# A linear-attention block on one core: a re-ordered head, later weight loads, and another column order for the folded kv product

## The chip, the cores and the metric

The kernel runs on one core of a Trainium2 chip. The metric is the device time of one execution in microseconds (us). A profiled execution also gives a span (first to last instruction); times are about 1.7 us longer than spans. The other cores are idle.

Every run also reports its mean granted TensorE clock (1.0 is full speed). For one core, a run is labelled slow only when it is over 1.5% above the fastest run of the same kernel; the means below use the other runs, called fast.

## The reference

Only the first block and the input of the second matter. S is 2048 tokens, D is 640, 32 heads of 20.

```python
xn = layernorm(x)                              # [2048, 640]
q, k, v = split(xn @ wqkv)                     # 32 heads of 20
pq, pk = phi(q), phi(k)                        # phi(t) = t+1 for t>0, else exp(t)
kv  = einsum("hsd,hse->hde", pk, v)            # 20 x 20 per head
den = einsum("hsd,hd->hs", pq, pk.sum(s))
o   = einsum("hqd,hde->hqe", pq, kv) / den
A   = o @ wo
B   = x + scatter(8 chosen tokens, gated MLP of them)   # chosen by x @ w_r
return x + A + B                               # block B on layernorm(x) too
```

The kernel never forms v or o. It accumulates G = xn^T pk over all tokens, gets kv from G and wv, keeps only the 20x20 blocks by a mask, and folds kv into wo: M = kv wo. The output is then pq M.

## The kernel before

Tokens come in 16 tiles of 128. For each tile t: load x, statistics (`ln_stats`), the power 0.5 on GpSimd, normalise (`ln_xn`), transpose (by TensorE for tiles 0 to 2, by DMA for the rest), key products `K(t)`, two activations `PHa`, a min-add `PHb` on VectorE, and the accumulation `G(t)`. I count tiles from 0.

```python
    def ln_mid(t, on_act=True):
        ...
        dve.tensor_scalar(out=t2[:], in0=MV[:, t, 1:2], scalar1=EPS_BF16, scalar2=None, op0=ALU.add)
        pool.tensor_tensor(out=s[:], in0=t2[:], in1=halfc[:], op=ALU.pow)
        ...
    def tr_dma(t):
        sp.dma_start_transpose(xnT[:, :, t * P : (t + 1) * P], XX[:, t, 0, :])
    def PHb(t):
        ek, rk = phis[t]
        dve.scalar_tensor_tensor(out=pk[:, t, :], in0=ek[:], scalar=1.0, in1=rk[:], op0=ALU.min, op1=ALU.add)
    ...
    def loads(t):                       # called at the end of iteration t, all on one queue but wo2
        if t < 5:
            ld(sp, XX[:, 6 + 2 * t : 8 + 2 * t, 1, :], x_v[:, 6 + 2 * t : 8 + 2 * t, :])
        if 5 <= t < 10:  ...            # one fifth of wq
        if 7 <= t < 12:  ...            # one fifth of wv
        if t == 9 or t == 10:  ...      # half of wo1
        if t == 13:  ...                # wg, in five
        if t == 14:  ...                # wu, in five
    ...
    def kv_ev(b0, b1):                  # mask kv on its way out of PSUM, columns re-ordered
        k1 = kv1[:].rearrange("p m g q -> p g q m")
        k2 = kv2[:].rearrange("p m g q -> p g q m")
        m1 = bm1[:].rearrange("p (q m) -> p q m", m=KC)
        for g in range(NG):
            src = PS[:, b0, g * GC : (g + 1) * GC] if g < 3 else PS[:, b1, 0:GC]
            dve.tensor_tensor(out=k1[:, g], in0=src.rearrange("p (q m) -> p q m", m=KC), in1=m1, op=ALU.mult)
        src = PS[:, b1, GC : 2 * GC].rearrange("p (q m) -> p q m", m=KC)
        for g in range(NG):
            dve.tensor_tensor(out=k2[:, g], in0=src, in1=bm2[:, g, :].rearrange("p (q m) -> p q m", m=KC), op=ALU.mult)

    def m_main(m, b, eng):              # one of five parts of M
        for h in range(2):
            for g in range(NG):         # narrow products: 32 output rows each
                pe.matmul(PS[32 * g : 32 * g + 32, b + h, 0:HW], lhsT=kv1[:, m, g, :], rhs=wo1[:, g, h * HW : (h + 1) * HW], ...)
            pe.matmul(PS[:, b + h, 0:HW], lhsT=kv2[:, m].rearrange("p g q -> p (g q)"), rhs=wo2[:, h * HW : (h + 1) * HW], ...)
        ...
    # ---- the order around the folding
    kv_pe(3, 6)
    kv_ev(3, 6)
    q_pe(0, 4, 1)                       # PE work that stands ahead of the first folded product
    q_fin(0, 3)
    zmask(4)
    q_pe(1, 0, 2)
    q_fin(0, 4)
    m_main(0, 6, dve)
```

## Time and profile before

131.05 us, median of three runs (130.75 to 131.63). The profiled run took 131.35 us with a span of 129.6 and a mean clock of 0.974.

| stretch (us from the span's start) | what | PE busy | VectorE busy |
|---|---|---|---|
| 0 to 27 | head, until the tiles follow each other freely | 21.6 of 27 | 20.4 |
| 27 to 57 | tile loop | 28.6 of 30 | 20.7 |
| 66 to 72 | masking of kv | 3.5 of 6 | 5.9 |
| 77 to 126 | rest of q, the output | all | 32.8 |

TensorE (PE) is the engine to feed. The key products of tiles 3, 4, 5, 6 and 15 start at 18.28, 22.01, 25.52, 28.19 and 54.00 us; when nothing waits, they are 2.67 us apart.

From the page of the kernel before: busy time of PE, then rows of 40 equal slices of the span (3.24 us each) in tenths of busy time; PEclk is the granted clock in tenths.

```profile
PE 117.0 (90%) x943; PEld 66.5 (51%) x943; DVE 90.5 (70%) x210; ACT 82.0 (63%) x184; POOL 21.9 (17%) x56
...
PE   6779887899998979999994799999999999999990
...
PEclk9986999999999999999999869999999999999999
DMA  3980068986487996999991000000000022222223
```

Counting slices from 0, PE has dents in slices 0 to 6 and in 21 and 22; around each there are two slices of lower clock (2 and 3, 22 and 23). The smaller dents in slices 12 and 14 are waits for late transposes in the loop. DMA is busy all through the loop, up to slice 20.

The waits of PE, from the view of who waited for whom (total us, times, longest):

```profile
PE PS L588 <- DVE kv L583: 2.5, 1, 2.5
PE PS L197 <- DMA xnT<-XX: 1.9, 3, 0.8
PE PS L174 <- DVE XX L167: 1.4, 2, 0.9
```

The largest is one wait of the first folded product (line 588) for the masking of kv (line 583). Key products (line 197) wait three times for DMA transposes. The view of the transposes' line gives their times from issue to landing:

```profile
DMA to landing us min/median/max: 2.6/2.9/4.6
```

The busy time per stretch puts the dents and the clock side by side. Columns: stretch, its length, busy us (and instructions) of PE, PE's weight loads, VectorE, ScalarE, GpSimd, then granted clock, DMA share and GB/s.

```profile
core 0: us, PE busy (x) PEld busy (x) DVE busy (x) ACT busy (x) POOL busy (x), PEclk, DMA share, GB/s
5.36:8.77 3.41, 1.54 (x12) 0.76 (x12) 2.96 (x12) 1.30 (x4) 0.56 (x1) 0.97 1.01 264
8.77:12.18 3.41, 3.41 (x17) 2.17 (x18) 3.08 (x11) 1.46 (x6) 0.55 (x1) 0.53 0.16 59
66.00:72.00 6.00, 3.53 (x46) 2.10 (x44) 5.92 (x9) 2.30 (x5) 0.00 (x0) 1.00 0.37 134
69.90:73.30 3.40, 1.29 (x12) 0.66 (x12) 3.40 (x7) 0.76 (x2) 0.00 (x0) 1.00 0.00 0
73.30:76.72 3.42, 3.42 (x34) 1.15 (x32) 2.80 (x10) 1.50 (x3) 0.21 (x1) 0.52 0.03 7
```

After 3.4 us in which PE was busy less than half the time (1.54 and 1.29 us), its clock is 0.53 and 0.52 in the next 3.4 us. (The stretches are cut by eye; under a_oldkv the halved ones are placed more exactly, at 8.54 and 73.40 us.) The groups of the folding (busy us, mean ns of one, idle time before):

```profile
L588 PE MATMUL PS<-wo,kv 128*32 128x320 bf16 x40 | 3.5, 337 | 2.5 <-DVE kv L583 2.5
L591 PE MATMUL PS<-wo,kv 128*128 128x320 bf16 x10 | 3.4, 337 | 0.0
L583 DVE TENSOR_TENSOR kv<-PS,bm 128x160 bf16<-128x160 f32 x4 | 3.2, 1083 | 0.0
L580 DVE TENSOR_TENSOR kv<-PS,bm 128x160 bf16<-128x160 f32 x4 | 3.0, 1050 | 0.2 <-PE PS L566 0.2
```

Eight multiplications of only 160 elements per partition take over 1 us each.

### The profile page before, as it was taken

Reading aid. Unit: us, or ns where it says so; the run is one execution under the profiler, and the core shown is the slowest. Engines: PE = TensorE matmul, PEld = TensorE weight load, DVE = VectorE, ACT = ScalarE, POOL = GpSimd, SP = SyncE. Lnnn points to the kernel's source line nnn. Section 1 sums busy time; section 2 is a strip of 40 time slices with the busy share of each in tenths; the row PEclk is TensorE's granted clock in tenths of the full one; section 3 lists DMA queues with packets and bytes.
Section 4 is the critical chain, followed back from the end, with each engine's and each line's share of the span. In section 5 each row is a group of like instructions: output and inputs, shape, how many; then the busy total and the mean of one; then the engine's idle time right before and its main releaser. Section 6 shows DMA issues by size and latency. Waiting matters only on the chain.

```text
span 129.6 us, 2638 instructions
## 1 busy us (share of the span) xinstructions
PE 117.0 (90%) x943; PEld 66.5 (51%) x943; DVE 90.5 (70%) x210; ACT 82.0 (63%) x184; POOL 21.9 (17%) x56
## 2 busy tenths in 40 slices
PE   6779887899998979999994799999999999999990
PEld 2246544466664546664572244464554565666660
DVE  1887987987999773247789954588568786855551
ACT  3055585868988674537946075788988879993000
POOL 7211337753332140000000014000000000000000
PEclk9986999999999999999999869999999999999999
DMA  3980068986487996999991000000000022222223
GB/s 89 347 223 0 0 149 201 162 199 135 94 216 168 223 248 110 333 364 413 309 347 37 5 3 0 0 8 3 0 0 5 0 108 94 106 101 104 101 101 101
DMA packets 20861, 16.87 MB, mean 130 GB/s; under 512 B 10512, under 2 KB 19568, under 8 KB 20848
## 3 DMA queue, kind: packets, MB, share of 16 engines
q1 hardware_dynamic: 18096, 15.24, 41.8%
q10 hardware_dynamic: 2752, 1.47, 4.4%
q8 instruction: 7, 0.11, 0.4%
q14 instruction: 6, 0.05, 0.1%
HBM read 11.80 MB, written 2.62 MB: 111 GB/s over the span
## 4 chain that ended last, share of the span: by engine, by line
PE 62%; DVE 20%; DMA 10%; ACT 2%; issue 2%; POOL 1%; SPq 0%; DVEq 0%; POOLq 0%; ACTq 0%
PE PS L664 18%; PE PS L447 16%; PE PS L197 8%; DMA xnT<-XX 7%; PE PS L228 4%; DVE pk L223 4%; DMA XX<-in_A_x_dram 3%; DVE XX L167 3%; DVE stats L143 3%; DVE kv L580 2%; DVE stats L141 2%; DVE kv L583 2%; PE PS L588 2%; PE PS L591 2%; PE PS L655 2%
## 5 line engine op out<-in xcount | busy, mean ns | idle before, releaser
L197 PE MATMUL PS<-wk,xnT 128*128 128x320 bf16 (+1 forms) x160 | 26.0, 311 | 3.6 <-DMA xnT<-XX 1.9
L447 PE MATMUL PS<-xnT,wq 128*128 128x512 bf16 x100 | 25.0, 389 | 0.0
L664 PE MATMUL PS<-Mb,pqT 128*128 128x320 bf16 x160 | 23.8, 300 | 0.0
L228 PE MATMUL PS<-pk,XX 128*128 128x512 bf16 x80 | 23.3, 379 | 0.5 <-DVE pk L223 0.5
L197 PEld LDWEIGHTS <-xnT 128*128 128x128 bf16 x160 | 15.6, 101 | 12.4 <-DMA xnT<-XX 3.8
L215 ACT ACTIVATE ek<-PS 128x320 bf16<-128x320 f32 x32 | 14.2, 444 | 12.2 <-PE PS L197 10.8
L223 DVE SCALAR_TENSOR_TENSOR pk<-ek,rk 128x640 bf16<-128x640 bf16 x16 | 13.1, 818 | 8.5 <-ACT rk L216 8.4
L453 ACT ACTIVATE qe<-PS 128x512 bf16<-128x512 f32 x20 | 11.9, 595 | 10.7 <-PE PS L447 6.5
L664 PEld LDWEIGHTS <-pqT 128*128 128x128 bf16 x160 | 14.7, 97 | 6.9 <-issue 0.2
L682 DVE TENSOR_TENSOR o<-PS,XX 128x640 bf16<-128x640 f32 x15 | 12.4, 824 | 7.8 <-PE PS L664 7.0
L459 DVE SCALAR_TENSOR_TENSOR pqT<-qe,qr 128x512 bf16<-128x512 bf16 x20 | 13.7, 694 | 2.3 <-ACT qr L454 2.1
L447 PEld LDWEIGHTS <-wq 128*128 128x128 bf16 x100 | 11.0, 120 | 8.4 <-issue 1.0
L216 ACT ACTIVATE rk<-PS 128x320 bf16<-128x320 f32 x32 | 14.3, 447 | 0.0
L153 POOL TENSOR_TENSOR s<-t,halfc 128x1 bf16<-128x1 bf16 x16 | 9.4, 586 | 27.5 <-DVE t L152 21.7
L233 PE MATMUL PS<-pk,XX 128*128 128x128 bf16 x64 | 14.0, 219 | 0.0
L190 ACT ACTIVATE XX<-XX,MR,SR 128x640 bf16<-128x640 bf16 x16 | 13.6, 913 | 0.0
L155 ACT ACTIVATE c<-XX,MV 128x640 bf16<-128x640 bf16 x13 | 11.1, 854 | 1.9 <-DVE MV L144 1.8
L228 PEld LDWEIGHTS <-XX 128*128 128x128 bf16 x80 | 7.8, 98 | 8.4 <-issue 0.3
L454 ACT ACTIVATE qr<-PS 128x512 bf16<-128x512 f32 x20 | 11.8, 591 | 0.0
L141 DVE BATCH_NORM_STATS2 stats<-XX 128x6 f32<-128x320 bf16 x16 | 7.8, 486 | 2.4 <-DMA XX<-in_A_x_dram 2.4
L143 DVE BATCH_NORM_STATS2 stats<-XX 128x6 f32<-128x320 bf16 x16 | 7.8, 485 | 0.0
L167 DVE TENSOR_SCALAR XX<-c,SR 128x640 bf16<-128x640 bf16 (+2 forms) x17 | 6.3, 377 | 1.5
(129 smaller groups left out, 122.9 us busy)
## 6 DMA issues: line engine op xcount, KB each, us to landing
out_dram<-o SPq DMA_DIRECT2D x15, 160.0 KB, 1.8
wg<-in_B_w_gate_dram SPq DMA_DIRECT2D x5, 384.0 KB, 4.7
wu<-in_B_w_up_dram SPq DMA_DIRECT2D x5, 384.0 KB, 7.9
wd<-in_B_w_down_dram SPq DMA_DIRECT2D x1, 1920.0 KB, 9.3
XX<-in_A_x_dram SPq DMA_DIRECT2D x5, 320.0 KB, 3.6
wk<-in_A_wqkv_dram ACTq DMA_DIRECT2D x2, 400.0 KB, 5.1
wq<-in_A_wqkv_dram SPq DMA_DIRECT2D x5, 160.0 KB, 2.7
wv<-in_A_wqkv_dram SPq DMA_DIRECT2D x5, 160.0 KB, 2.8
```

Source lines behind the costliest of these rows:

```text
L190: act.activation(XX[:, t, 1, :], XX[:, t, 1, :], AF.Identity, bias=MR[:, t : t + 1], scale=SR1[:, t : t + 1])
L197: pe.matmul(PS[:, b + h, 0:w], lhsT=xnT[:, kc, t * P : (t + 1) * P], rhs=wk[:, kc, h * HW : h * HW + w], start=(kc == 0), stop=(kc == KC - 1),
L215: act.activation(ek[:, sl], PS[:, b + h, 0:HW], AF.Exp)
L216: act.activation(rk[:, sl], PS[:, b + h, 0:HW], AF.Relu)
L223: dve.scalar_tensor_tensor(out=pk[:, t, :], in0=ek[:], scalar=1.0, in1=rk[:], op0=ALU.min, op1=ALU.add)
L228: pe.matmul(PS[:, a, :], lhsT=lhsT, rhs=pk[:, t, 0:512], start=(t == 0), stop=(t == T - 1),)
L233: pe.matmul(PS[:, 5, a * P : (a + 1) * P], lhsT=lhsT, rhs=pk[:, t, 512:D], start=(t == 0 and a == 0), stop=(t == T - 1), skip_group_check= ...
L447: pe.matmul(PS[:, bank, :], lhsT=by5(wq[:, kc, :])[:, m, :], rhs=xnT[:, kc, tb * TBLK : (tb + 1) * TBLK], start=(kc == 0), stop=(kc == KC ...
L453: act.activation(e, PS[:, bank, :], AF.Exp)
L459: dve.scalar_tensor_tensor(out=pqT[:, m, tb * TBLK : (tb + 1) * TBLK], in0=e, scalar=1.0, in1=r, op0=ALU.min, op1=ALU.add,)
L664: pe.matmul(PS[:, b + h, 0:HW], lhsT=pqT[:, kc, t * P : (t + 1) * P], rhs=Mb[:, kc, h * HW : (h + 1) * HW], start=False, stop=(kc == KC - ...
L682: dve.tensor_tensor(out=ot[:].rearrange("p (h c) -> p h c", h=2), in0=PS[:, b : b + 2, 0:HW], in1=XX[:, t, 1, :].rearrange("p (h c) -> p h ...
```

## The change

The intent: keep kv in natural column order, so that its masking is three contiguous instructions, and let the folded product read its weights with a step of five columns instead; keep weight loads out of the loop, where they meet the DMA transposes; normalise tile 0 before the statistics of tile 1, transpose tile 3 by PE too, and put small filler products into PE's gaps so that its clock stays up. Smaller parts: `w_r` is loaded as five rows and transposed by PE instead of as a column of 2-byte pieces, and a copy of the mean disappears by storing the statistics in the upper half of float32 words.

```diff
     def kv_ev(b0, b1):
-        (eight multiplications with a re-ordered output, as above)
+        dve.tensor_tensor(out=kv1[:, 0:3, :], in0=PS[:, b0, 0 : 3 * GC].rearrange("p (g c) -> p g c", c=GC),
+                          in1=bm1[:].unsqueeze(1).to_broadcast([P, 3, GC]), op=ALU.mult)
+        dve.tensor_tensor(out=kv1[:, 3, :], in0=PS[:, b1, 0:GC], in1=bm1[:], op=ALU.mult)
+        dve.tensor_tensor(out=kv2[:], in0=PS[:, b1, GC : 2 * GC].unsqueeze(1).to_broadcast([P, NG, GC]),
+                          in1=bm2[:], op=ALU.mult)
     def m_main(m, b, eng):
         for h in range(2):
             for g in range(NG):
-                pe.matmul(..., lhsT=kv1[:, m, g, :], ...)
+                pe.matmul(..., lhsT=by5(kv1[:, g, :])[:, m, :], ...)
-            pe.matmul(PS[:, b + h, 0:HW], lhsT=kv2[:, m].rearrange("p g q -> p (g q)"), ...)
+        for h in range(2):
+            pe.matmul(PS[:, b + h, 0:HW], lhsT=by5(kv2[:].rearrange("p g c -> p (g c)"))[:, m, :], ...)

     def loads(t):
         if t < 5:  ...                                   # x, unchanged
-        (wq, wv, wo1, wo2 in pieces at t = 5 to 11; wg at 13; wu at 14)
+        if t == 13:                                      # behind the last tr_dma(15)
+            ld(sp, wq[:], ...); ld(sp, wv[:], ...); ld(sp, wo1[:], ...); (wo2, wg, wu)

+    (head written out by hand; its start)
+    ln_xn(0, ((0, 3 * P), (3 * P, D)))
+    warm(1, 256)                                         # filler products of 256 columns
+    tr_pe(0, 0, act, act)
+    warm(3, 256)
     ln_stats(1, 0)
-    ln_xn(0, ((0, 3 * P), (3 * P, D)))
-    tr_pe(0, 0, act, act)
...
+    warm(3, 256)
+    tr_pe(1, 2, act, act)
...
+    tr_pe(3, 3, act, act)                                # tile 3 by PE, before by DMA
... (cut: w_r by rows, MVf, where constants are made)
```

More of the change, by code (lines that the diff above doesn't have):

```diff
@@ L90 @@
     rbf = st([P, T], BF16, "rbf")
-    MV = st([P, T, 2], BF16, "MV")
+    MVf = st([P, T, 2], F32, "MVf")
+    MV = MVf[:].bitcast(BF16).rearrange("p t (k o) -> p t k o", o=2)[:, :, :, 1]
     SR = st([P, T], F32, "SR")
@@ L104 @@
     dve.memset(zero[:], 0.0)
+    dve.memset(MVf[:], 0.0)
     ld(act, wk[:, :, 0:HW], wqkv_v[:, :, D : D + HW])
@@ L107, with warm @@
     ld(act, wk[:, :, HW:D], wqkv_v[:, :, D + HW : 2 * D])
-    with nc.allow_non_contiguous_dma(reason="one column"):
-        ld(act, wk[:, :, D : D + 1], B_w_r.rearrange("(kc p o) -> p kc o", p=P, o=1))
+    wr = st([KC, P], BF16, "wr")
+    ld(act, wr[:], B_w_r.rearrange("(kc p) -> kc p", p=P))
     for t in range(2, 4):
         ld(sp, XX[:, t, 1, :], x_v[:, t, :])
-    def warm(n):
+    def warm(n, w=512):
         for _ in range(n):
-            pe.matmul(PS[:, 7, :], lhsT=zero[:, 0:P], rhs=zero[:], start=True, stop=True)
+            pe.matmul(PS[:, 7, 0:w], lhsT=zero[:, 0:P], rhs=zero[:, 0:w], start=True, stop=True)
     warm(10)
@@ L129, in tok @@
                   allow_small_or_imprecise_dtypes=True)
+    dve.memset(bm2[:], 0.0)
     dve.memset(one11[:], 1.0)
@@ L154, in ln_mid @@
         if on_act:
-            act.activation(c[:], XX[:, t, 1, :], AF.Identity, bias=MV[:, t, 0:1], scale=-1.0)
+            act.activation(c[:], XX[:, t, 1, :], AF.Identity, bias=MVf[:, t, 0:1], scale=-1.0)
         else:
-            nm = tmp.tile([P, 1], F32, tag="nm", name="nm", bufs=2)
-            dve.tensor_scalar(out=nm[:], in0=MV[:, t, 0:1], scalar1=1.0, scalar2=None, op0=ALU.mult)
-            dve.tensor_scalar(out=c[:], in0=XX[:, t, 1, :], scalar1=nm[:], scalar2=-1.0,
+            dve.tensor_scalar(out=c[:], in0=XX[:, t, 1, :], scalar1=MVf[:, t, 0:1], scalar2=-1.0,
                               op0=ALU.subtract, op1=ALU.mult)
@@ L186, in xpx_cols @@
         dve.tensor_scalar(out=SR1[:], in0=SR[:], scalar1=1.0, scalar2=None, op0=ALU.add)
-        dve.scalar_tensor_tensor(out=MR[:], in0=MV[:, :, 0], scalar=-1.0, in1=SR[:], op0=ALU.mult, op1=ALU.mult)
+        dve.scalar_tensor_tensor(out=MR[:], in0=MVf[:, :, 0], scalar=-1.0, in1=SR[:], op0=ALU.mult, op1=ALU.mult)
     def xpx(t):
@@ L275, in consts_a, with consts_e @@
             )
+        for j in range(1, 4):
+            ld(sp, hm[32 * j : 32 * j + 32, :], hm[0:32, :])
+    def consts_e():
+        pool.memset(bm2[0:E2, 0, :], 1.0)
+        band(bm2[0:E2, 0, :], P, 8)
+        for g in range(1, NG):
+            ld(sp, bm2[32 * g : 32 * g + 32, g, :], bm2[0:E2, 0, :])
     def consts_b():
-        for j in range(1, 4):
-            ld(act, hm[32 * j : 32 * j + 32, :], hm[0:32, :])
         pool.memset(sel32[:, 0, :], 0.0)
@@ L291, in consts_c @@
         band(bm1[:], 0, 8)
-    def consts_e():
-        pool.memset(bm2[:], 0.0)
-        pool.memset(bm2[0:E2, 0, :], 1.0)
-        band(bm2[0:E2, 0, :], P, 8)
-    def consts_f():
-        for g in range(1, NG):
-            ld(act, bm2[32 * g : 32 * g + 32, g, :], bm2[0:E2, 0, :])
     def consts_d():
         pool.iota(lowkey[:], pattern=[[-P, T]], base=LOW, channel_multiplier=-1)
-    pool_extra = {1: lambda: tok(0, 512), 2: consts_b, 3: consts_c, 4: consts_e, 5: lambda: (consts_f(), consts_d()),
-                  6: lambda: tok(512, 1024), 7: lambda: tok(1024, 1536), 8: lambda: tok(1536, S)}
+    pool_extra = {3: consts_b, 4: consts_c, 5: consts_d, 6: lambda: tok(0, 512),
+                  7: lambda: tok(512, 1024), 8: lambda: tok(1024, 1536), 9: lambda: tok(1536, S)}
     wo_v = A_wo.rearrange("(g r) d -> r g d", r=GC)
@@ L314, in loads @@
             ld(sp, XX[:, 6 + 2 * t : 8 + 2 * t, 1, :], x_v[:, 6 + 2 * t : 8 + 2 * t, :])
-        if 5 <= t < 10:
-            k = t - 5
-            ld(sp, wq[:, k, :], wqkv_v[:, k, 0:D])
-        if 7 <= t < 12:
-            k = t - 7
-            ld(sp, wv[:, k, :], wqkv_v[:, k, 2 * D : 3 * D])
-        if t == 9 or t == 10:
-            h = 2 * (t - 9)
-            ld(sp, wo1[:, h : h + 2, :], wo_v[0:P, h : h + 2, :])
-        if t == 11:
+        if t == 13:
+            ld(sp, wq[:], wqkv_v[:, :, 0:D])
+            ld(sp, wv[:], wqkv_v[:, :, 2 * D : 3 * D])
+            ld(sp, wo1[:], wo_v[0:P, :, :])
             for g in range(NG):
-                ld(act, wo2[32 * g : 32 * g + 32, :], A_wo[GC * g + P : GC * (g + 1), :])
-        if t == 13:
+                ld(sp, wo2[32 * g : 32 * g + 32, :], A_wo[GC * g + P : GC * (g + 1), :])
             for k in range(KC):
                 ld(sp, wg[:, k, :], wg_v[:, k, :])
-        if t == 14:
             for k in range(KC):
@@ L338 @@
     ln_mid(0, False)
+    ln_xn(0, ((0, 3 * P), (3 * P, D)))
+    warm(1, 256)
+    tr_pe(0, 0, act, act)
+    warm(3, 256)
     ln_stats(1, 0)
-    ln_xn(0, ((0, 3 * P), (3 * P, D)))
-    tr_pe(0, 0, act, act)
     ln_stats(1, 1)
     ln_mid(1, False)
+    consts_e()
     ld(act, XX[:, 4:6, 1, :], x_v[:, 4:6, :])
-    ln_xn(1)
-    ln_stats(2, 0)
-    for t in range(T):
-        if t == 0:
-            K(0, (0,), 4)
-            PHa(0, (0,), 4)
-            tr_pe(1, 2, dve, act)
-            K(0, (1,), 4)
-            ln_stats(2, 1)
-            ln_mid(2, False)
-            PHa(0, (1,), 4)
-            rcopy(0, 5)
-            ln_stats(3, 0)
-            ln_xn(2)
-            K(1)
-            PHa(1, (0,))
-            ln_stats(3, 1)
-            tr_pe(2, 0, dve, act)
-            PHa(1, (1,))
-            rcopy(1)
-            ln_mid(3)
-            PHb(0)
-            ln_stats(4, 0)
-        else:
-            if t > 1:
-                K(t)
-            if t > 2:
-                PHb(t - 1)
-            if t + 2 < T:
-                ln_xn(t + 2)
-                tr_dma(t + 2)
-            if t == 1:
-                PHb(1)
-            else:
-                PHa(t)
-                rcopy(t)
-            if t + 3 < T:
-                ln_stats(t + 3, 1)
-                ln_mid(t + 3)
-            if t + 4 < T:
-                ln_stats(t + 4, 0)
-            if t == 2:
-                G(0)
-            if t >= 2:
-                G(t - 1)
-        if t in pool_extra:
-            pool_extra[t]()
@@ new lines @@
+    loads(0)
+    K(0, (0,), 4)
+    pe.transpose(PS[:, 3, :].bitcast(BF16)[:, 0:KC], wr[:], ident[0:KC, 0:KC])
+    act.copy(wk[:, :, D], PS[:, 3, :].bitcast(BF16)[:, 0:KC])
+    PHa(0, (0,), 4)
+    ln_stats(2, 0)
+    ln_xn(1)
+    warm(3, 256)
+    tr_pe(1, 2, act, act)
+    K(0, (1,), 4)
+    ln_stats(2, 1)
+    ln_mid(2, False)
+    PHa(0, (1,), 4)
+    rcopy(0, 5)
+    K(1, (0,))
+    ln_stats(3, 0)
+    ln_xn(2)
+    PHa(1, (0,))
+    tr_pe(2, 0, act, act)
+    K(1, (1,))
+    PHa(1, (1,))
@@ new lines @@
+    rcopy(1)
+    ln_stats(3, 1)
+    ln_mid(3, False)
+    K(2, (0,))
+    ln_stats(4, 0)
+    ln_xn(3)
+    tr_pe(3, 3, act, act)
+    K(2, (1,))
+    PHb(0)
+    ln_stats(4, 1)
+    PHa(2, (0,))
+    ln_mid(4)
+    PHb(1)
+    ln_stats(5, 0)
+    PHa(2, (1,))
+    rcopy(2)
+    ln_xn(4)
+    tr_dma(4)
+    loads(1)
+    G(0)
+    K(3)
+    ln_stats(5, 1)
+    ln_mid(5)
+    PHb(2)
+    ln_stats(6, 0)
+    G(1)
+    ln_xn(5)
+    tr_dma(5)
+    loads(2)
+    PHa(3)
+    rcopy(3)
+    ln_stats(6, 1)
@@ L392 @@
+    ln_mid(6)
+    ln_stats(7, 0)
+    G(2)
+    loads(3)
+    for t in range(4, T):
+        K(t)
+        PHb(t - 1)
+        if t + 2 < T:
+            ln_xn(t + 2)
+            tr_dma(t + 2)
+        PHa(t)
+        rcopy(t)
+        if t + 3 < T:
+            ln_stats(t + 3, 1)
+            ln_mid(t + 3)
+        if t + 4 < T:
+            ln_stats(t + 4, 0)
+        G(t - 1)
+        if t - 1 in pool_extra:
+            pool_extra[t - 1]()
         loads(t)
@@ L435 @@
     zm = st([P, KC, 32], BF16, "zm")
-    kv1 = st([P, KC, NG, 32], BF16, "kv1")
-    kv2 = st([P, KC, NG, 32], BF16, "kv2")
+    kv1 = st([P, NG, GC], BF16, "kv1")
+    kv2 = st([P, NG, GC], BF16, "kv2")
     Mb = st([P, KC, D + 1], BF16, "Mb", "wkM")
@@ L574, in kv_ev @@
     def kv_ev(b0, b1):
-        k1 = kv1[:].rearrange("p m g q -> p g q m")
-        k2 = kv2[:].rearrange("p m g q -> p g q m")
-        m1 = bm1[:].rearrange("p (q m) -> p q m", m=KC)
-        for g in range(NG):
-            src = PS[:, b0, g * GC : (g + 1) * GC] if g < 3 else PS[:, b1, 0:GC]
-            dve.tensor_tensor(out=k1[:, g], in0=src.rearrange("p (q m) -> p q m", m=KC), in1=m1, op=ALU.mult)
-        src = PS[:, b1, GC : 2 * GC].rearrange("p (q m) -> p q m", m=KC)
-        for g in range(NG):
-            dve.tensor_tensor(out=k2[:, g], in0=src, in1=bm2[:, g, :].rearrange("p (q m) -> p q m", m=KC), op=ALU.mult)
+        dve.tensor_tensor(out=kv1[:, 0:3, :], in0=PS[:, b0, 0 : 3 * GC].rearrange("p (g c) -> p g c", c=GC),
[3 more added lines that the diff above has]
+                          in1=bm2[:], op=ALU.mult)
     def m_main(m, b, eng):
@@ L587, in m_main @@
             for g in range(NG):
-                pe.matmul(PS[32 * g : 32 * g + 32, b + h, 0:HW], lhsT=kv1[:, m, g, :],
+                pe.matmul(PS[32 * g : 32 * g + 32, b + h, 0:HW], lhsT=by5(kv1[:, g, :])[:, m, :],
                           rhs=wo1[:, g, h * HW : (h + 1) * HW],
                           start=True, stop=False, skip_group_check=True)
-            pe.matmul(PS[:, b + h, 0:HW], lhsT=kv2[:, m].rearrange("p g q -> p (g q)"),
+        for h in range(2):
+            pe.matmul(PS[:, b + h, 0:HW], lhsT=by5(kv2[:].rearrange("p g c -> p (g c)"))[:, m, :],
                       rhs=wo2[:, h * HW : (h + 1) * HW],
```

## The prediction

> **What bounds the kernel now.** The matmul engine: the chain of waits gives PE 62% of the 129.6 us span, VectorE 20%, DMA 10%. Busy time per stretch shows four stages: a head until the tile loop runs freely (to 27 us), the tile loop (PE busy 28.6 of 30 us), the folding of kv into wo (66 to 72 us: PE busy 3.5 us, VectorE 5.9), and a tail from 77 us in which PE is never idle and which the change leaves alone. Work to win:
>
> 1. Head. The key products of the fourth to seventh tiles start at 18.3, 22.0, 25.5 and 28.2 us by the timeline; unhindered, tiles follow every 2.67 us. PE waits for VectorE and DMA transposes, and the granted clock is 0.53 from 8.77 to 12.18 us, after 3.4 us with PE busy only 1.54.
> 2. Loop. Two transposes come late (PE waits 0.6 and 0.8 us at 42.3 and 48.7 us, with lost pace about 1.7 us); they took up to 4.6 us to land, median 2.9, while weights loaded on the same queue.
> 3. kv. Eight 128x160 multiplications of about 1.08 us (5.9 us on VectorE); PE idles 2.5 us before the first folded product, then the clock is 0.52 from 73.3 to 76.7 us, after 3.4 us with PE busy 1.29. [...]
>
> **What the change does, costed.**
> - kv: three instructions of 480, 160 and 640 elements. Contiguous PSUM multiplications of 512 and 640 elements take 0.69 and 0.82 us here, so I estimate 1.7 us in place of 5.9. The old output stepped 256 B per element[...]. PE has 2.6 us of other products queued meanwhile: its wait vanishes, minus 2.5 us, and so does the clock drop, minus 1.7 (half of 3.4). The folded product's weights become strided; their loads (0.09 us) stay mostly hidden: plus 0.2.
> - Loop: no weights, no late transpose: minus 1.7 us. 6.4 MB then start near 44 us; at the 330 to 410 GB/s seen they end near 61 us, wq first, well before its use near 55.
> - Head: the first tile is normalised before the second's statistics (0.5 us sooner), the column load of 2-byte pieces goes, the fourth tile is transposed by PE (plus 0.35 us PE, 0.73 us ScalarE copies). Walking the new order through with this trace's durations, the fifth tile's products start at 19.7 us in place of 22.0, the seventh's at 25.1 in place of 28.2: minus 3.1 us. Fillers add 0.8 us of PE work in idle time; I expect them to soften the clock drop, not surely to remove it.
>
> All lies on the critical path: 3.1+1.7+2.5+1.7-0.2 = 8.8 us. Allowing some loss in the head: **122.5 us, range 119.5 to 126.0**. Faster by over 2%: 0.95; within 2%: 0.04; slower: 0.01.
>
> **What would show it.** kv multiplications near 1.7 us, no PE wait for them, clock 1.0 around 70 us; loop transposes landing in about 2.9 us with no PE wait; the seventh tile's products at 25 us; the later tail unchanged; DMA near idle in the loop, near full from 44 to 66 us.
>
> **What would make it wrong.** wq or wv late, as 6.4 MB stand in one queue; the copy of the routing keys (5.6 us now) stuck behind weights[...]; ScalarE bounding the new head (3.0 us per tile with transposes' copies); the clock window falling so that the head stays at half speed.

3.1+1.7+2.5+1.7-0.2 = 8.8 us off 131.05 leaves 122.3, and some loss in the head makes it 122.5. That the clock drop would go with PE's wait was the estimate from the one trace, where both slow stretches last 3.41 us and follow one with PE busy less than half the time. The clock window that the text names is measured under a_oldkv, the lower speed at the start of a head (up to 10.22 us in b_kv) just ahead of it.

## The result, and the profile after

123.15 us, median of four runs (122.81 to 124.20), against 131.22 for four runs of the kernel before. The ratio is 0.940 (95% interval 0.933 to 0.947). Ratios here are the mean time of one kernel's fast runs over that of the other's of the same rounds, so not quite the ratio of the quoted medians.

The profiled run took 123.06 us: span 121.4, mean clock 1.0.

| | before | after |
|---|---|---|
| key products of tile 4, 6, 15 start | 22.01, 28.19, 54.00 | 20.72, 26.44, 50.47 |
| first q product | 60.4 | 56.85 |
| first folded product | 72.01 | 66.00 |
| span | 129.6 | 121.4 |

The span fell by 8.2 us: 1.75 by tile 6, 1.78 more in the loop (25.81 us from tile 6 to tile 15 became 24.03), 2.48 more by the first folded product, 2.2 after it.

From the page of the kernel after (slices are 3.04 us now):

```profile
PE 113.3 (93%) x945; PEld 66.3 (55%) x956; DVE 87.0 (72%) x203; ACT 82.3 (68%) x188; POOL 21.7 (18%) x55
...
PE   5978898999999999999999999999999999999980
...
PEclk9999999999999999999999999999999999999999
DMA  3961309993225343899999970000000222322222
```

The second dent is gone, the clock never falls, and DMA is light in the loop (slices 9 to 15) and full from slice 16 to 23, some 49 to 72 us. The waits of PE:

```profile
PE PS L175 <- DVE XX L168: 1.5, 4, 0.5
PE PS L118 <- DVE zero L105: 1.3, 1, 1.3
PE PS L198 <- DMA xnT<-XX: 0.7, 2, 0.5
```

The wait for kv is gone. Waits for transposes are down to two, both for the first DMA transposes (tiles 4 and 6). Landing times, from the view of the transposes' line:

```profile
DMA to landing us min/median/max: 2.6/2.7/4.3
```

Busy time per stretch, the same two head stretches, then the masking and what follows it:

```profile
5.36:8.77 3.41, 2.90 (x19) 1.36 (x17) 2.92 (x11) 1.21 (x5) 1.27 (x4) 1.00 0.71 209
8.77:12.18 3.41, 2.67 (x25) 1.83 (x25) 3.20 (x12) 2.96 (x11) 1.13 (x3) 1.00 0.22 75
62.50:65.00 2.50, 2.45 (x42) 1.65 (x41) 2.29 (x5) 0.56 (x2) 0.00 (x0) 1.00 1.04 401
65.00:68.40 3.40, 3.40 (x30) 1.56 (x28) 2.44 (x10) 2.21 (x5) 0.00 (x0) 1.00 1.06 387
```

Groups of the folding:

```profile
L603 PE MATMUL PS<-wo,kv 128*32 128x320 bf16 x40 | 2.4, 315 | 0.0
L607 PE MATMUL PS<-wo,kv 128*128 128x320 bf16 x10 | 2.3, 316 | 0.0
...
L597 DVE TENSOR_TENSOR kv<-PS,bm 128x640 bf16<-128x640 f32 x1 | 0.8, 816 | 0.0
...
L594 DVE TENSOR_TENSOR kv<-PS,bm 128x480 bf16<-128x480 f32 x1 | 0.7, 658 | 0.2 <-PE PS L585 0.2
```

With the third one (160 elements, 325 ns) the masking takes 1.80 us in place of 6.2. The folded products themselves also got shorter (2.4+2.3 us busy in place of 3.5+3.4, some of the latter at half clock), which I had not predicted.

### The profile page after: what moved, and what is told of

Read it like the earlier page. It is cut to its first block, busy times and chain, and to the rows that moved or that the text cites. A ratio compares the mean times of both kernels' runs of the same rounds, so it can differ in the third digit from the quotient of the medians.

```text
span 121.4 us, 2635 instructions
## 1 busy us (share of the span) xinstructions
PE 113.3 (93%) x945; PEld 66.3 (55%) x956; DVE 87.0 (72%) x203; ACT 82.3 (68%) x188; POOL 21.7 (18%) x55
## 4 chain that ended last, share of the span: by engine, by line
PE 75%; DVE 11%; DMA 6%; POOL 4%; issue 2%; ACT 0%; DVEq 0%
PE PS L680 19%; PE PS L466 18%; PE PS L198 11%; PE PS L229 9%; POOL s L156 4%; DMA xnT<-XX 4%; PE PS L234 3%; DVE XX L168 2%; DVE stats L146 2%; DMA XX<-in_A_x_dram 2%; PE PS L603 2%; PE PS L607 2%; PE PS L671 2%; PE PS L626 1%; PE PS L488 1%
## 5 line engine op out<-in xcount | busy, mean ns | idle before, releaser
L198 PE MATMUL PS<-wk,xnT 128*128 128x320 bf16 (+1 forms) x160 | 24.8, 300 | 1.0 <-DMA xnT<-XX 0.7
L466 PE MATMUL PS<-xnT,wq 128*128 128x512 bf16 x95 | 23.8, 382 | 0.5 <-issue 0.4
L229 PE MATMUL PS<-pk,XX 128*128 128x512 bf16 x74 | 22.3, 379 | 0.0
L198 PEld LDWEIGHTS <-xnT 128*128 128x128 bf16 x160 | 15.1, 97 | 8.4 <-DMA xnT<-XX 1.4
L156 POOL TENSOR_TENSOR s<-t,halfc 128x1 bf16<-128x1 bf16 x16 | 10.1, 632 | 25.0 <-DVE t L155 25.0
L158 ACT ACTIVATE c<-XX,MVf 128x640 bf16<-128x640 bf16 x12 | 10.3, 862 | 1.3 <-DVE MVf L147 1.3
```

The lines of the kernel that those rows point to most:

```text
L198: pe.matmul(PS[:, b + h, 0:w], lhsT=xnT[:, kc, t * P : (t + 1) * P], rhs=wk[:, kc, h * HW : h * HW + w], start=(kc == 0), stop=(kc == KC - 1),
L229: pe.matmul(PS[:, a, :], lhsT=lhsT, rhs=pk[:, t, 0:512], start=(t == 0), stop=(t == T - 1),)
L466: pe.matmul(PS[:, bank, :], lhsT=by5(wq[:, kc, :])[:, m, :], rhs=xnT[:, kc, tb * TBLK : (tb + 1) * TBLK], start=(kc == 0), stop=(kc == KC ...
```

## The experiments

Twelve kernels ran, in three calls, each call on one chip beside runs of the kernel before; all gave correct results. Names starting with a_ derive from the kernel after, those with b_ from the kernel before. A thirteenth idea, to compute the power 0.5 on VectorE instead of GpSimd, did not compile.

| call | kernel | mean us (runs) | ratio to before | clocks |
|---|---|---|---|---|
| 1 | a_oldkv | 127.09 (4) | 0.978 | 0.981, 0.986, 1.0, 1.0 |
| 1 | a_oldkv_fill | 126.27 (4) | 0.972 | 0.995 to 1.0 |
| 1 | a_kv8 | 123.08 (4) | 0.947 | 0.995 to 1.0 |
| 1 | a_loopw | 124.70 (4) | 0.961 | 0.998 to 1.0 |
| 2 | a_nofill | 123.47 (6) | 0.943 | 0.982, 0.995, four 1.0 |
| 2 | a_hinter | 124.50 (6) | 0.951 | 0.999 to 1.0 |
| 2 | a_xearly | 122.70 (6) | 0.938 | 0.995 to 1.0 |
| 2 | a_phb | 123.07 (6) | 0.940 | 0.994 to 1.0 |
| 3 | after_again | 123.36 (7) | 0.942 | 0.995 to 1.0 |
| 3 | a_xearly_again | 122.50 (6) | 0.936 | 0.998 to 1.0 |
| 3 | b_kv | 125.59 (5 of 6) | 0.959 | 0.995 to 1.0 (slow run 0.986) |
| 3 | b_kv_late | 124.61 (6) | 0.953 | three 0.986, three 0.999 to 1.0 |

In call 1 a single run of the kernel before took 128.76 us, against 130.4 to 131.8 for the six others, so that the 95% intervals there are wide (0.963 to 0.992 for a_oldkv) and three of the others count as slow. That run explains itself: its clock was 1.0. Over the three calls the fast runs of the kernel before are

| mean clock | runs | mean us |
|---|---|---|
| 1.0 | 1 | 128.76 |
| 0.987 | 15 | 130.46 |
| 0.974 | 8 | 131.36 |

(One more, at 0.961, took 131.69.) One halved stretch of 3.41 us lowers the mean clock of a 129 us span by 0.5 x 3.41/129, which is 0.013; so these are runs with no, one and two such stretches. The first costs 1.7 us (resting on the one run without any), the second 0.9. Which of the two places the single stretch fell in is not recorded for these runs.

The mean clock has two limits, which the clock records in the packed traces show. Time before the first record counts as full speed, though products ran slower there: in b_kv, whose first record begins at 10.22 us, the five key products that start at 7.60 us took 1.51 us; in the kernel before, whose first record begins at 5.14, they took 0.85. And a halved stretch that begins after PE's last product counts although it costs nothing: from 120.0 us in a_phb, where PE's work ends at 117.9. The means of 0.994 to 0.997 of the profiled runs are of this kind. Below, "no halved stretch" means none between the first record and the end of PE's work.

### a_oldkv: only the old folding put back

```diff
-    kv1 = st([P, NG, GC], BF16, "kv1")      # likewise kv2, kv_ev, m_main
+    kv1 = st([P, KC, NG, 32], BF16, "kv1")  # all four as in the kernel before
```

> The changed kernel with the old folding put back (kv1, kv2, their eight multiplications and the order of the folded products as before); head, loads and fillers new. Theory: the folding alone is worth the PE wait (2.5 us), the clock drop after it (1.7 us) and a shorter folded product (about 0.5 us): the time goes from 123.15 to 127.5 (126.8 to 128.2), with a PE wait near 2.5 us at 66 to 69 us and a stretch of about 3.4 us at clock 0.5 right after. Rival: the folding only filled time that the earlier stages now give anyway (VectorE reaches it earlier, PE has other products): then under 124.5.

Measured 127.09, 4.0 us over a_kv8 of the same call, which runs like the kernel after. The waits of PE in a_oldkv:

```profile
PE PS L607 <- DVE kv L602: 2.5, 1, 2.5
```

The wait is back. The halved clock, though, is not always. Busy time per stretch of the profiled run, the wait and what follows:

```profile
66.00:69.40 3.40, 0.94 (x9) 0.36 (x7) 3.40 (x6) 1.64 (x4) 0.00 (x0) 1.00 1.04 374
69.40:72.80 3.40, 3.40 (x45) 1.55 (x44) 3.33 (x12) 1.26 (x3) 0.00 (x0) 1.00 0.97 325
```

PE was busy only 0.94 of 3.4 us and the clock stayed at 1.0; two other runs of the four have mean clocks of 0.981 and 0.986, as one halved stretch gives. So the idle time makes a halved stretch possible, and something else decides. The clock records in the packed traces (start, length and granted share of each stretch) suggest what. In the trace of the kernel before, the mean clock from 8 to 9 us is 0.77 and from 73 to 74 us 0.70, which at half clock puts the starts of the two slow stretches at 8.54 and 73.40 us; they are 64.86 us apart, 19.0 times 3.413, the length of each of the two in the clock records: windows of that length seem to follow one another as a grid. Such a grid can cut one idle time of 2.5 us in two, and the clock records show that it did so here. In all 14 kept traces every stretch at full clock is a whole number of windows: 119.47 us in a_oldkv is 35.0, 61.44 in the kernel before 18.0, 116.05 in the kernel after 34.0. So the grid is known in runs without a drop, too. In the kernel before, the wait for kv lies in one window but for its first 0.46 us; in a_oldkv a boundary at 68.17 us cuts it in two halves. PE busy in these windows, first the kernel before, then a_oldkv:

```profile
69.99:73.40 3.41, 1.39 (x13) 0.73 (x13) 3.41 (x7) 0.67 (x2) 0.00 (x0) 1.00 0.02 5
```

```profile
64.75:68.17 3.42, 2.16 (x19) 1.20 (x17) 3.42 (x6) 2.17 (x4) 0.00 (x0) 1.00 1.03 386
68.17:71.58 3.41, 2.21 (x19) 1.00 (x18) 3.41 (x7) 0.04 (x1) 0.00 (x0) 1.00 1.07 363
```

My expectation of a halved stretch "right after" was too firm.

### a_oldkv_fill: the same, with PE kept busy through the wait

```diff
     q_fin(0, 4)
+    warm(12)                                # twelve filler products of 512 columns
     m_main(0, 6, dve)
```

> As a_oldkv, with twelve filler products of 512 columns (0.216 us each, 2.6 us) queued on PE ahead of the first folded product, so that PE waits about as long for the same VectorE work but is never idle. Theory: the clock drop is a cost of its own, brought on by PE's idle time: the clock stays at 1.0 and the time is about 1.7 us under that of a_oldkv (near 125.8). Rival: the clock falls there for another reason, or the drop costs nothing as other engines bound that stretch: the same time as a_oldkv.

126.27, with all four runs within 126.23 to 126.34 and all clocks at 0.995 or more. In the profiled run the twelve fillers take 2.75 us from 65.66 us on (0.216 us from one to the next, with 0.38 for the last), and PE has no idle time there:

```profile
65.60:68.40 2.80, 2.80 (x18) 1.13 (x15) 2.80 (x5) 1.09 (x2) 0.00 (x0) 1.00 1.06 370
```

The fillers take 0.8 us off the mean of a_oldkv, not 1.7, because in two of its four runs there was no halved stretch to avoid. Those two are 126.32, as long as with the fillers, and 127.36, where the profile shows a wait of 1.3 us for a DMA transpose in the head; the two with a halved stretch took 127.20 and 127.47. So the drop looks like a cost of its own, of about 1 us in these two runs (neither was profiled, so another cause in them is not excluded). With PE work in the gap it came in none of four runs, without it in two of four: this fits the theory, and four runs are few.

### a_kv8: natural order, but eight instructions

```diff
-        (three multiplications of 480, 160 and 640 elements)
+        for g in range(NG):
+            src = PS[:, b0, g * GC : (g + 1) * GC] if g < 3 else PS[:, b1, 0:GC]
+            dve.tensor_tensor(out=kv1[:, g, :], in0=src, in1=bm1[:], op=ALU.mult)
+        for g in range(NG):
+            dve.tensor_tensor(out=kv2[:, g, :], in0=PS[:, b1, GC : 2 * GC], in1=bm2[:, g, :], op=ALU.mult)
```

> The changed kernel, natural column order kept, but the kv multiplications as eight instructions of 160 elements instead of three. Theory: the old price was the output's 256 B step, not the count: each of the eight takes about 0.33 us (as the single 160-element one does in the changed kernel), some 2.1 us in all, PE does not wait for them, and the time stays within 0.4% of the changed kernel (123.2). Rival: eight small instructions each carry their large cost: near 1 us each, and a PE wait of over 1.5 us.

123.08, no different from the kernel after. Its multiplications, from the view of that tile (min/median/max ns):

```profile
L596 DVE TENSOR_TENSOR kv<-PS,bm x4: 315/320/325, 62.7 to 63.6; 128x160 bf16<-128x160 f32 x4
L598 DVE TENSOR_TENSOR kv<-PS,bm x4: 313/314/315, 63.8 to 64.5; 128x160 bf16<-128x160 f32 x4
```

The same count, the same sizes, contiguous: 0.32 us each against 1.05 to 1.08. The inputs are read in the same order in both, so the output step of 256 B was the price, not the number of instructions. Why that step costs so much was not shown.

### a_loopw: the weights back in the loop

```diff
-        if t == 13:
-            ld(sp, wq[:], ...); ld(sp, wv[:], ...); ld(sp, wo1[:], ...); ...
+        (wq, wv, wo1, wo2 in pieces at t = 5 to 11, wg at 13, wu at 14, as before)
```

> The changed kernel with the loads of q, v and wo weights put back into the loop (and wu an iteration later), as before. Theory: transposes in the loop land late again (up to 4.6 us), PE waits for them once or twice, and the time rises by about 1.7 us, to 124.9 (124.3 to 125.5). Rival: with the loop starting sooner and PE transposes for four tiles there is slack, or the late transposes came from elsewhere: under 123.8.

124.70: 1.6 us over a_kv8 of the same call, as the theory had it. The waits of PE, and the landing times in its transposes' view:

```profile
PE PS L198 <- DMA xnT<-XX: 1.8, 3, 0.9
```

```profile
DMA to landing us min/median/max: 2.6/3.5/4.7
```

The median landing rises from 2.7 to 3.5 us, and PE waits three times. One of the waits (0.65 us at 46.1) is late in the loop, the other two are in the head; in the profiled run, the quickest of the four (124.03), tile 6 to tile 15 takes 25.15 us against 24.03. Whether weights and transposes meet in the queue or in the DMA engines, this run does not tell.

### a_nofill: no filler products

```diff
-    warm(1, 256)
     tr_pe(0, 0, act, act)
-    warm(3, 256)
...
-    warm(3, 256)
     tr_pe(1, 2, act, act)
```

> The changed kernel without the seven filler products of 256 columns in the head. Theory: without them PE is idle over half of some 3.4 us window near 6 to 9 us, and in part of the runs, by where the window falls, the clock is halved for 3.4 us in the head (mean clock near 0.986 in those runs); such a run is 0.5 to 1.5 us longer, the mean over the runs 0.3 to 1.0 us above the changed kernel (123.2). Rival: the tighter head keeps the clock by itself and the fillers do nothing, or they delay PE: mean within 0.2 us or lower, clock 1.0 in all runs.

123.47, which cannot be told from the kernel after (123.33 and 123.36). In the profiled run the clock did drop in the head:

```profile
5.30:8.70 3.40, 1.73 (x12) 0.78 (x11) 3.06 (x11) 1.51 (x5) 1.27 (x4) 1.00 0.76 241
8.70:12.10 3.40, 3.14 (x15) 2.02 (x16) 3.19 (x13) 1.65 (x6) 1.12 (x4) 0.51 0.15 48
```

That run took 123.95 us (clock 0.982); the other five had 0.995 or more, and one of them took 124.11. So the fillers, 0.75 us of PE work in idle time, probably ward off a halved stretch that without them came in one run of six; what they are worth on average lies below what these runs can tell (0.3 to 1.0 us was expected). Besides the eleven runs of the kernel after, the 32 runs of the variants with fillers and the new folding show no such drop either (lowest clock 0.994). On the grid of this run the window from 5.33 to 8.74 us had PE busy for 1.70 us; in the ten traces with fillers no full-clock window that begins before 14 us had less than 2.30.

### a_hinter: only the order of the folded products put back

```diff
                 (four narrow products)
-        for h in range(2):
             (one full product)
```

> The changed kernel with only the order of the folded products put back: four narrow products and one full product per half, half after half, instead of eight narrow ones and then two full ones. In the traces a folded part (ten products) takes 0.98 us in the old order and layout and 0.81 us in the new. Theory: the order does it, as each change between narrow and full products costs about 0.08 us: parts of 0.98 us or a little more, and a time 0.85 us longer (124.0). Rival: the layout of the weights does it: 0.81 us a part and the same time.

124.50, 1.14 us over after_again; the ratios to before are 0.951 and 0.942. The groups, with strided weights in both:

```profile
L603 PE MATMUL PS<-wo,kv 128*32 128x320 bf16 x40 | 3.4, 332 | 0.0
L606 PE MATMUL PS<-wo,kv 128*128 128x320 bf16 x10 | 3.3, 332 | 0.0
```

By the chain of waits a part of ten products takes 1.07 us in this order (0.27+0.27+0.27+0.26), 0.98 in the kernel before at full clock (0.25+0.24+0.25+0.24: old order, contiguous weights), 0.81 in the kernel after (0.41+0.40). So the order is worth 0.26 us a part, and the strided weights cost 0.09 where the order doesn't hide them: a load takes 0.11 to 0.12 us there, 0.09 to 0.10 with contiguous weights. The expected 0.98 us a part and 124.0 us left out that second cost. This is the part of the change that I had booked as plus 0.2 us.

### a_xearly, after_again and a_xearly_again: all loads of x in the head

```diff
-    loads(0)
+    for i in range(5):
+        loads(i)
     K(0, (0,), 4)
...
-    loads(1)                                # likewise loads(2), loads(3), loads(4), behind transposes
```

> The changed kernel with all five remaining loads of x queued in the head right after the first, ahead of the first DMA transpose, instead of one behind each transpose. Theory: the fifth to seventh tiles' transposes land late (3.9 to 5.0 us against 2.6)[...]: landing falls to about 2.7 us, PE no longer waits for them, the seventh tile's key products start near 25.5 instead of 26.4 us, and the time falls by 0.5 to 1.0 us (122.4). Rival: VectorE bounds the head, the waits for the transposes only show its lateness: within 0.2 us.

122.70, but the kernel after had not run in that call. So both ran side by side:

> The changed kernel itself, as the measure for the three kernels run beside it. 123.2 us (122.8 to 123.7), clock over 0.99 in all runs, while most runs of the kernel before show 0.987 or 0.974 (one or two halved stretches of 3.4 us).

> The kernel with all loads of x in the head, run again beside the changed kernel, since they were not on the same chip. Theory (loads of x delay the transposes a little): 0.4 to 0.7 us under the changed kernel. Rival (nothing is gained, the lower time came from the chip or from the landing of the first tile): within 0.2 us of it.

123.36 against 122.50: 0.86 us, more than expected, and the ranges do not overlap (123.02 to 124.05 in seven runs, 121.95 to 122.92 in six). This version beats both kernels. In the profiled runs of a_xearly_again the key products of tile 6 start at 26.07 without a wait, in after_again at 27.42 after waiting 1.35 us for their transpose (landing up to 5.0 us). But that profiled run is the slowest of its seven (124.05). Over the profiled runs this wait is 0.21 us in the kernel after, 0.37 in a_hinter, 0.54 in a_oldkv_fill, 0.88 in a_kv8, 0.92 in a_loopw, 1.28 in a_oldkv and 1.35 in after_again, 0.79 on average; both runs with x early have none. (a_nofill and a_phb have none either; there PE came later, after other waits.) The average is near the measured gain. PE still waits for tile 4's transpose in both (0.49 and 0.34 us), so the loads of x are not what delays that one; what does is open.

### a_phb: the min-adds behind the normalisation

```diff
-    PHb(1)
     ln_stats(5, 0)
     ...
     ln_xn(4)
     tr_dma(4)
+    PHb(1)
...                                          # PHb(2) likewise behind tr_dma(5)
```

> The changed kernel with the min-add of the second and third tile's keys on VectorE moved behind the normalisation of the fifth and sixth tile. In the traces the GpSimd power of the fifth and sixth tile takes 1.06 us where it runs beside that min-add, and 0.55 to 0.62 elsewhere. Theory: these 0.45 us lie on the head's chain (statistics, power, reciprocal, normalisation, transpose): the powers go back to about 0.6 us, the fifth tile's transpose is issued 0.4 to 0.8 us sooner, and the time falls by 0.3 to 0.6 us. Rival: what bounds the head from there on is VectorE's total work, which is the same: the powers get shorter, the time stays within 0.2 us.

123.07, 0.3 us under the mean of the kernel after in another call: not shown to be faster. The powers did get shorter. Timelines of GpSimd, first the kernel after, then a_phb (start, duration):

```profile
15.09 1.06 POOL L156 TENSOR_TENSOR s<-t,halfc 128x1 bf16<-128x1 bf16 x1 [2.27 <-DVE t L155]
17.76 1.06 POOL L156 TENSOR_TENSOR s<-t,halfc 128x1 bf16<-128x1 bf16 x1 [1.61 <-DVE t L155]
```

```profile
14.78 0.55 POOL L156 TENSOR_TENSOR s<-t,halfc 128x1 bf16<-128x1 bf16 x1 [2.27 <-DVE t L155]
17.77 0.55 POOL L156 TENSOR_TENSOR s<-t,halfc 128x1 bf16<-128x1 bf16 x1 [2.44 <-DVE t L155]
```

In the kernel after, a min-add with two SBUF inputs runs from 14.92 to 15.74 and another from 17.59 to 18.40, and the powers end 0.41 us after them. In the kernel before, the power that starts at 13.56 us, under a min-add from 13.39 to 14.20, takes 1.06 us, too. These three, of the 32 powers in the two traces, are the ones that start while a min-add runs; those that start ahead of one and overlap it (at 20.50 us, before a min-add at 20.66, in the kernel after) take 0.55 to 0.57. Why was not shown. Tile 4's transpose was issued at 16.14 instead of 16.87, though 0.46 us of this is only an earlier start of the profiled run (first key product at 6.86 instead of 7.32). PE then waited 1.2 us for a min-add that had been moved too far back. What VectorE gives to one it takes from the other, as the rival said; with that new wait in it the run does not prove the rival, either.

### b_kv and b_kv_late: the change built up from the kernel before

```diff
 b_kv:       kv1, kv2, kv_ev, m_main of the kernel after in the kernel before
 b_kv_late:  b_kv, and loads(t) of the kernel after
```

> The kernel before with the folding in natural order as the only change. Theory: the folding is independent of the rest, so it takes off the 2.5 us wait, the halved stretch that follows it (1.7 us where it falls) and about 0.7 us of the shorter folded parts: 131.1 goes to 126.6 (125.9 to 127.3); mean clock near 0.987 at most, one halved stretch in the head. Rival (gains overlap, PE would wait for something else): above 128.

> The kernel before with the folding in natural order and the q, v and wo weights loaded after the last transpose; head as before, no fillers. Theory: the late loads take 1.4 to 1.8 us off b_kv: 125.0 (124.3 to 125.7), and the rest up to the changed kernel, 1.8 us, is the head with its fillers, of which about 1 us is the halved stretch there. Rival: with the old head the loop is late by itself and the loads hide in it: within 0.5 us of b_kv.

With the kernel before at 130.82 (the mean of that call's eleven runs), the steps are

| step | mean us | gain |
|---|---|---|
| before | 130.82 | |
| + folding (b_kv) | 125.59 | 5.2 |
| + late weights (b_kv_late) | 124.61 | 1.0 |
| + head and fillers (after_again) | 123.36 | 1.25 |
| + x early (a_xearly_again) | 122.50 | 0.86 |

The folding gave more than expected, the late weights less, though that step mixes two things: the runs of b_kv_late at full clock (123.99, below) are 1.6 us under b_kv, as much as a_loopw lost. Five of six runs of b_kv have no halved stretch, where the kernel before has one or two in all but one of its runs; this fits the wait for kv as the cause of the usual one. Of b_kv_late, three runs at clock 0.999 to 1.0 took 123.8 to 124.3 (mean 123.99), three at 0.986 took 125.0 to 125.4 (125.23): so the clock still drops in half of the runs, for 1.25 us. That it drops in the head is inferred: the profiled run is one without a drop, but there the wait for kv is gone. b_kv has the same head and shows the drop in one of its six runs. Of the last step's 1.25 us, then, about half (123.99 to 123.36) is a shorter head at full clock, and the rest is the clock. The head's other edits (tile 0 first, tile 3 by PE, `w_r` by rows, statistics in place) were not tried one by one.

## Why the prediction was right or wrong

The time (122.5 predicted, 123.15 measured), the class and most gains were right in kind. The sum was right partly by luck, as two of its terms erred in opposite directions: the head was to give 3.1 us and gave 1.25, the folded products were to cost 0.2 and gained 0.85.

- **The wait for kv, minus 2.5 us: right.** It is gone from the kernel after, and a_oldkv brings it back at 2.5. The masking takes 1.80 us against my 1.7, and a_kv8 shows that the output's step was its price.
- **The clock after it, minus 1.7 us: right that it goes, too firm in size and kind.** The kernel before shows 1.7 us between runs with one halved stretch and the single run without; a_oldkv against a_oldkv_fill shows about 1. And a_oldkv, with the same wait, dropped in only two of four runs; where the wait falls on the window's grid decides, as far as two traces show (PE busy 1.39 of 3.41 us and a halved clock in the kernel before, 2.16 and 2.21 and none in a_oldkv), and a prediction should have called it an average.
- **The folded products, plus 0.2 us: wrong in sign.** I looked at the strided weights only. The change also groups the narrow products, and that weighs more: 0.17 us a part, 0.85 us in five parts, as a gain. With it the folding sums to 2.5+1.7+0.85 = 5.05 us; b_kv measured 5.2 (the 1.7 in this sum is the figure that rests on one run).
- **The loop, minus 1.7 us: right in the traces (1.78 us between tile 6 and tile 15), 1.0 us in the build-up (1.6 between runs at full clock) and 1.6 us when undone.** No transpose is late in the loop any more, DMA is light there, and the 6.4 MB of weights came in time: wq was issued at 47.5, landed in 5.2 us and was first needed at 56.85. The copy of the routing keys took 4.9 us to land instead of 5.6; the feared delay behind the weights did not come.
- **The head, minus 3.1 us: right in direction, mis-sized.** The step that failed is "Walking the new order through with this trace's durations, the fifth tile's products start at 19.7 us in place of 22.0, the seventh's at 25.1". They started at 20.72 and 26.44, and the whole step measured 1.25 us, of which only about 0.6 is a shorter head. The walk gave each DMA transpose the median landing of 2.9 us; in the profiled runs of the kernel after, tile 4's was waited for until 3.85 us after its issue, and the slowest took 4.3 and 5.0. Moving the loads of x ahead took 0.86 us off in a_xearly_again, and tile 6's wait was gone there; tile 4's stayed. The rest of the head is VectorE's: it is busy 22.1 of the first 27 us after the change, 20.4 before. That this work bounds it is argued from that figure and from a_phb, and not shown by itself.
- **The fillers "to soften the clock drop, not surely to remove it"**: no drop in eleven runs of the kernel after, nor in 32 runs of variants with them; one in six without, in the new head; four in twelve in the old one (b_kv and b_kv_late; by the mean clock, the place not profiled).
- **The later tail unchanged: right.** From the routing products (line 550 before, 569 after) to the end it is 45.3 us before and 45.4 after.

## What to carry to other kernels

When VectorE writes a small tile with a large step so that TensorE can read it contiguously, try it the other way round: here the step cost VectorE a factor of over three and cost each of TensorE's weight loads some 0.02 us, 0.09 us per ten products where it was not hidden. An idle gap of TensorE can cost more than its length: in the trace of the kernel before, a wait of 2.5 us was followed by a clock of 0.50 for 3.41 us, and over its runs a halved stretch went with 0.9 to 1.7 us more. Read the mean clock of every run before comparing times, and count its losses as an average over runs. In a walk through a new order, give DMA transposes the range of landing times that the trace shows, not its median.

## What the runs measured of the hardware

- A gap of 2.5 us was followed by a halved clock in the trace of the kernel before. On the grids of the 14 kept traces, once the clock was up, every window with PE busy for up to 1.39 of 3.41 us was followed by a halved clock (seven windows with some work, six of them at a kernel's end), none with 1.94 or more was, and of four with 1.59 to 1.70 two were.
- Drops inside a kernel vary from run to run: the kernel before had no, one or two halved stretches, at 128.76, 130.46 and 131.36 us, a spread of 2%. The same wait of 2.5 us was followed by a halved clock where most of it lay in one window, and was not where a boundary cut it in halves (a_oldkv).
- Narrow (32-column) and full products that alternate every half took 1.07 us per ten products of 320 columns (a_hinter), grouped 0.81 (kernel after).
- 160 bf16 elements from PSUM took VectorE 0.32 us contiguous (a_kv8) and 1.05 to 1.08 with a step of 256 B (kernel before), which is over 6 ns per element.
- A power of one element per partition on GpSimd took 1.06 us where it started while a two-input min-add ran on VectorE (kernel after), and 0.55 where that had been moved away (a_phb).
- No run here says why tile 4's DMA transpose, issued at 16.3 to 17.2 us, was waited for until 3.5 to 4.4 us after its issue in nine profiled runs with the new head, where the median landing is 2.6 to 3.5, with loads of x right behind it (kernel after) or without (a_xearly).
